# Reordering the opening of a filter-and-MLP kernel: filter spreads on VectorE, a fifth product on GpSimd, no filler matmuls, and M computed later

## The chip, the cores and the metric

The kernel runs on one core of one Trainium2 chip. The metric is the device time of an execution in microseconds (us). Lower is better. A profiled execution also gives a span, from its first instruction to its last, and times inside it are counted from the start of the span.

Engines are named as in the profile: PE is TensorE's matmul, PEld its weight load, DVE is VectorE, ACT is ScalarE, POOL is GpSimd, SP is SyncE.

## The reference

```python
# x (8, 3072, 256); filt_r, filt_i (1537, 256)
X = np.fft.rfft(x, axis=1)
Y = X * (filt_r + 1j * filt_i)[None]
y = np.fft.irfft(Y, n=3072, axis=1).reshape(24576, 256)
# w1, w2 (256, 1024); w_out (1024, 256)
g = np.maximum(y @ w1, y @ w2)
out = g @ w_out
```

Eight sequences are filtered along their length in the frequency domain, and every token of the result goes through a two-matrix maximum and an output matrix. All inputs and the output are float32.

## The kernel before

**The whole.** A transform of 3072 points is done as two short transforms by matrix products (128 points, called stage S1, then 24 points, S2), with a product by the filter between S2 and S3, and the way back as S3 and S4. The maximum is rewritten: `max(a, b) = relu(a - b) + b`, so the kernel needs `Wd = w1 - w2`, and `M = w2 @ w_out` for the part without the relu. The MLP takes tiles `tt` of 512 tokens, 6 for each of the 8 sequences. In the main loop (from line 719) each tile has eight steps; a step issues one hidden block (`moe_h`), one piece of the output of the tile before (`moe_o`), and what a table of steps (`plan`) puts there of the transforms of later sequences.

**The opening.** Before the main loop, lines 589 to 663 build the tables (sine tables `C1`, `G1`, `U`, `VP`, `VQ`; filter `F`; `Wd`, `M`) and transform sequence 0 without a trip through DRAM. The order there is written out by hand: a manual schedule keeps every engine's instructions in program order, and the engines wait for each other by semaphores. The change lies in this part alone. Its pieces:

- `load_f` brings the real (`ri` 0) and the imaginary (`ri` 1) half of the filter into `Fs`, by a DMA on POOL's queue. `expand_f(g, ri, E)`, a **spread**, copies group g of `Fs` by 8 to 12 matmuls into PSUM (`pf`), and engine E casts it into `F`. There are 8 groups with two halves each, 16 spreads.
- `first_s1(c, E)` is S1 for sixth c of the sequence: 8 matmuls into `pa`, evacuated by E into `At`. Before them come two **spins**, matmuls of zeros whose result nobody reads.
- `first_t1(g, V)` transposes part g of `At` into `pt`, and V (DVE) copies it to `bt`. It needs all six S1 tiles.
- `first_s2(g, pool)` makes two PSUM tiles `px` and multiplies both by `F` into `pq`, two products. DVE does both, or with `pool` set ACT copies the second tile to SBUF (`xs`) and POOL multiplies it.
- `first_s3(g, pq)` issues one spin and 32 small matmuls into `pz`, and ACT evacuates to `Zt`. With `split` ACT and DVE take half each.
- `tables_pe` (16 transposes of `U`, DVE copies to `VP`), `tables_q(h, S)` (`VQ` from `VP`), `table_g` (`G1` from `C1`), `fix_f` (POOL corrects group 0 of `F`).
- `prep_wd(k)` is POOL work: k 0 casts w2 to `w2b`, k 1 and 2 make the halves of `Wd`. `prep_w(k)` with k 0 and 1 transposes `w2b` into `w2T`; with k 2 and 3 it makes the halves of `M` in a PSUM tile `pm` by 8 matmuls each, and DVE evacuates `pm` after the second.
- `first_t2h(E, h)` transposes the first piece of `Zt` into `zr`; then `s4(0)`, line 661, needs `zr` and `G1`, and the main loop starts.

**PSUM.** In the opening two tags share it: `pa` with 2 slots of two banks, `px` with 4 slots of one bank. `bank2(...)` takes a `pa` slot. A spread for ACT takes one `pa` slot, a spread for DVE two `px` slots; `pt` of `first_t1`, `px` and the split `pz` take `px` slots. A matmul into a slot waits until its former tile has been read.

**The loop of the opening.** `order` is (1, 2, 3, 4, 5, 0, 6, 7). Pass n issues S2 of its group, the transposes of the group three passes on, a spread, and S3 of the group two passes back.

Of the kernel before, what the change touches and what calls it, by code (L numbers as in the profile page):

```python
# [8 lines left out]
FP32 = mybir.dt.float32  # L9
BF16 = mybir.dt.bfloat16  # L10
# [5 lines left out]
D = 256  # L16
# [13 lines left out]
def kernel(  # L30
# [26 lines left out]
    V, S, G, TE = nc.vector, nc.scalar, nc.gpsimd, nc.tensor  # L57
# [26 lines left out]
    p2 = setup.enter_context(tc.tile_pool(name="p2", bufs=2, space=bass.MemoryType.PSUM))  # L84
# [3 lines left out]
    def bank2(shape, dtype, name, tag=None):  # L88
        if tag is None:
            ring.append(ring.pop(0))  # L90
            tag = ring[-1]
        return p2.tile(shape, dtype, tag=tag, name=name)
# [20 lines left out]
    def expand_f(g, ri, E):  # L113
        if E is V:
            pf = [p2.tile([128, 2, D], FP32, tag="px", name="pf", bufs=4) for _ in range(2)]
        else:
            p_ = bank2([128, 2, 2, D], FP32, "pf")
            pf = [p_[:, b] for b in range(2)]
        fs = Fs[ri]
        for b in range(2):  # L120
            for c in range(2):
                m = 4 * b + c
                TE.matmul(pf[b][64 * c:64 * c + 32], Sel[:, m], fs[:, 2 * g:2 * g + 2], start=True, stop=True)
                p0 = 64 * c + 32
                if g:
                    TE.matmul(pf[b][p0:p0 + 32], Sel[:, 7 - m], fs[:, 16 - 2 * g:14 - 2 * g:-1], start=True, stop=True)  # L126
                else:
                    TE.matmul(pf[b][p0:p0 + 32, 0], Sel[:, 7 - m + c], fs[:, 0], start=True, stop=True)
                    TE.matmul(pf[b][p0:p0 + 32, 1], Sel[:, 7 - m], fs[:, 15], start=True, stop=True)
        f_ = F[:, ri, :, 2 * g:2 * g + 2].rearrange("p b u d -> p b (u d)")  # L130
        if E is V:
            for b in range(2):
                V.tensor_copy(f_[:, b], pf[b].rearrange("p u d -> p (u d)"))
        else:
            evac(E, f_, p_.rearrange("p b u d -> p b (u d)"))
# [145 lines left out]
    def sines_u(q):  # L281
        Uv = U.rearrange("p t (r x) -> p t r x", r=2)
        if q < 2:
            S.activation(Uv[:, :, :, 12 * q:12 * q + 12], uu[:, q], AF.Sin, bias=zero, scale=TWO_PI)
        else:
            for dr in range(2):
                S.activation(Uv[:, 0, dr, 0:24].rearrange("p (q j) -> p q j", q=2), uu[:, :, 0, dr], AF.Sin, bias=zero,
                             scale=mk[:, dr:dr + 1])
# [6 lines left out]
    def tables_pe():  # L295
        pv = bank2([128, 16, 2, 64], BF16, "pv")
        for u in range(16):
            TE.transpose(pv[:, u], U[:, 2 * u:2 * u + 2].rearrange("p c x -> p (c x)"), I128)
        V.tensor_copy(VP[:, :, :, 0:48], pv[:, :, :, 0:48])

    def table_g():
        pg = bank2([128, 128], BF16, "pg")
        TE.transpose(pg, C1, I128)
        S.activation(G1, pg, AF.Copy)

# [13 lines left out]
    def spin(pd, n):  # L319
        for _ in range(n):  # L320
            TE.matmul(pd, Sp, Sp.rearrange("p (o x) -> p o x", o=1).to_broadcast([128, 4, 128]), start=True, stop=True)

    def prep_wd(k, w1f, w2f):
        if k == 0:
            for dc in range(2):
                G.tensor_copy(w2b[:, dc], w2f[:, dc])
        else:
            G.tensor_tensor(Wd[:, k - 1], w1f[:, k - 1], w2f[:, k - 1], OP.subtract)
# [4 lines left out]
    pm_ = []  # L333

    def prep_w(k, E):
        if k < 2:
            pt = bank2([128, 4, D], BF16, "pt")
            for ji in range(4):
                for dc in range(2):
                    TE.transpose(pt[:, ji, 128 * dc:128 * dc + 128],  # L340
                                 w2b[:, dc, 128 * (4 * k + ji):128 * (4 * k + ji) + 128], I128)
            evac(E, w2T[:, 4 * k:4 * k + 4], pt)
            return
        if k == 2:
            pm_.append(bank2([128, 2, D], FP32, "pm"))
        for j in range(8):
            TE.matmul(pm_[0][:, k - 2], w2T[:, j, 128 * (k - 2):128 * (k - 2) + 128], Wo[:, j],
                      start=(j == 0), stop=(j == 7))
        if k == 3:
            evac(E, M, pm_[0])  # L350
# [88 lines left out]

    def first_s1(c, E):  # L440
        pa = bank2([128, 2, 2, 2, 4, T], FP32, "pa")
        spin(pa[:, 0].rearrange("p b a n t -> p (b a n t)"), 2)
        for dh in range(2):
            for n in range(4):
                TE.matmul(pa[:, dh, :, :, n], xb[0, c][:, n, 128 * dh:128 * dh + 128],
                          Ct.rearrange("p (b a t) -> p b a t", b=2, a=2), start=True, stop=True)
        evac(E, At[:, :, 0:48].rearrange("p h (a n) t -> p h a (n t)", a=2)[:, :, :, 128 * c:128 * c + 128],
             pa.rearrange("p h b a n t -> p (h b) a (n t)"))

    def first_t1(g, E):  # L450
        pt = p2.tile([128, 2, 2, D], BF16, tag="px", name="pt", bufs=4)
        t0 = 8 * (g // 2) + 2 * (g % 2)
        for c in range(2):
            for i in range(2):
                for dh in range(2):
                    TE.transpose(pt[:, c, i, 128 * dh:128 * dh + 128],
                                 At[:, 2 * dh:2 * dh + 2].rearrange("p b m t -> p t (b m)")[:, t0 + 4 * c + i], I128)
        o = bt[0][0:ROWS, 8 * (g // 2):8 * (g // 2) + 8].rearrange("p (c u) d -> p c u d", c=2)[:, :, 2 * (g % 2):2 * (g % 2) + 2]
        evac(E, o.rearrange("p c u d -> p c (u d)"), pt[0:ROWS].rearrange("p c u d -> p c (u d)"))

    def evac(E, out_, in_):
        if E is V:
            V.tensor_copy(out_, in_)
        else:
            S.activation(out_, in_, AF.Copy)  # L465

    def first_s2(g, pool):
        px = [p2.tile([128, 2, D], FP32, tag="px", name="px", bufs=4) for _ in range(2)]
        for i in range(2):
            for k, c in QUADS:  # L470
                t_ = 8 * (g // 2) + 4 * c + 2 * (g % 2) + i
                TE.matmul(px[k][64 * c:64 * c + 64, i], U[64 * k:64 * k + 48, 4 * g + 2 * i + c],
                          bt[0][64 * k:64 * k + 48, t_], start=True, stop=True)
        if pool:
            xs = apool.tile([128, 2, D], FP32, tag="at", name="xs")
            S.activation(xs[0:FROWS], px[1][0:FROWS], AF.Copy)
        pq = []
        for k in range(2):
            pq.append(pqpool.tile([128, 2, 2, D], BF16, tag="pq", name="pq"))
            E, src = (G, xs) if k and pool else (V, px[k])  # L480
            E.tensor_tensor(pq[k][0:FROWS],  # L481
                            src[0:FROWS].rearrange("p (o i) d -> p o i d", o=1).to_broadcast([FROWS, 2, 2, D]),
                            F[0:FROWS, :, k, 2 * g:2 * g + 2], OP.mult)
        return g, pq
# [115 lines left out]
    wf = load_w()  # L600
    load_wo()
    for c in range(6):
        load_x(1, c)
    spin(bank2([128, 2, 512], FP32, "pd")[:, 0], 24)
    order = (1, 2, 3, 4, 5, 0, 6, 7)
    expand_f(1, 0, S)
    expand_f(2, 0, S)
    first_s1(0, S)
    expand_f(3, 0, V)
    first_s1(1, S)  # L610
    sines_u(0)
    expand_f(4, 0, V)
# [4 lines left out]
    expand_f(0, 0, V)  # L617
    first_s1(4, V)
    first_s1(5, S)
    sines_u(2)  # L620
    first_t1(1, V)
    first_t1(2, V)
    expand_f(6, 0, S)
    table_g()
    tables_pe()
    expand_f(1, 1, S)
    first_t1(3, V)
    expand_f(2, 1, S)
    pend = []
    for n, g in enumerate(order):  # L630
        pend.append(first_s2(g, n in (0, 1, 3, 6)))
        if n < 5:
            first_t1(order[n + 3], V)
        if n < 6:
            expand_f((0, 3, 4, 5, 6, 7)[n], 1, S)
        if n in (1, 3):
            tables_q(n // 2, S)
        if n == 5:
            expand_f(7, 0, S)
        if n == 1:  # L640
            fix_f()
        if n in (3, 4, 6):
            prep_wd((3, 4, 6).index(n), *wf)
        if n > 5:
            prep_w(n - 6, V)
        if n > 1:
            first_s3(*pend.pop(0))
    prep_w(2, V)
    first_s3(*pend.pop(0))
    prep_w(3, V)  # L650
    first_s3(*pend.pop(0), split=True)
    zr[0] = zrpool.tile([128, N2, D], BF16, tag="zr", name="zr")
    first_t2h(V, 0)
    first_t2h(S, 1)
# [64 lines left out]
    for tt in range(6 * B + 1):  # L719
        b, i = divmod(tt, 6)  # L720
# [40 lines left out]
```

## Time and profile before

| | us |
|---|---|
| median of 6 runs | 539.84 |
| lowest, highest | 538.28, 543.79 |
| profiled execution, its own time | 538.28 |
| its span | 536.5 |
| opening, to the first matmul of `s4(0)` | 51.66 |
| main loop, from there to the end of the span | 484.84 |

The profiled execution is the fastest of the six, 1.56 us below the median, and 1.8 us of its own time lie outside the span. Busy shares of the whole span are PE 95%, ACT 63%, DVE 60% and POOL 14%. In the list of groups a row has the line, the engine, the operation, output and inputs with shapes, a count, busy time, mean ns of one, and the idle time ahead of them. In the timeline a row has a start, a duration, the engine, the line, and in brackets how long the engine had been idle and who released it.

### The profile page before, as it was taken

How to read it: one execution, taken by the hardware profiler on the slowest of the kernel's cores; microseconds unless marked ns; L12 is line 12 of the kernel's file. 1: busy time of each engine (PE TensorE's matmuls, PEld its weight loads, DVE VectorE, ACT ScalarE, POOL GpSimd, SP SyncE). 2: the span in 40 equal slices, each digit the busy share in tenths (PEclk: the TensorE clock that was granted, in tenths of full speed). 3: DMA queues.
4: the chain of work that ended last, by engine and by line, in shares of the span. 5: the costliest groups of instructions: out<-in, count | busy, mean ns of one | idle time of the engine just before them, and what ended most of it. 6: DMA issues, size and time to landing. Idle time of an engine off the chain costs nothing.

```text
span 536.5 us, 12166 instructions
## 1 busy us (share of the span) xinstructions
PE 510.8 (95%) x5135; PEld 347.1 (65%) x5213; DVE 323.5 (60%) x433; ACT 336.0 (63%) x594; POOL 74.7 (14%) x126
## 2 busy tenths in 40 slices
PE   8887999999999999999999899999999999999995
PEld 3545666666666666676667566676666666677774
DVE  8686679435863577438763677447863678443432
ACT  6685757865786578755775467755676556544540
POOL 7294011011101200021001200021000000000000
PEclk9999999999999999999999999999999999999998
DMA  8972496879678956699378966599367936421122
GB/s 156 285 131 42 142 174 147 200 237 196 138 233 215 202 155 176 172 223 210 99 228 199 199 148 163 159 222 220 115 188 205 159 106 160 118 89 77 42 80 79
DMA packets 67740, 87.06 MB, mean 162 GB/s; under 512 B 4002, under 2 KB 48292, under 8 KB 66596
## 3 DMA queue, kind: packets, MB, share of 16 engines
q1 hardware_dynamic: 52196, 44.84, 38.1%
q0 software_dynamic: 15488, 41.43, 29.3%
q8 instruction: 41, 0.67, 0.5%
q14 instruction: 15, 0.12, 0.1%
HBM read 53.74 MB, written 47.19 MB: 188 GB/s over the span
## 4 chain that ended last, share of the span: by engine, by line
PE 69%; DMA 5%; DVE 1%; issue 1%; ACT 0%; SPq 0%
PE po L572 27%; PE ph L547 23%; PE po L567 7%; PE pz L401 4%; DMA bt<-ad 3%; PE px L420 3%; PE py L531 3%; PE pa L366 3%; DMA ad<-at 2%; DVE pq L425 1%; ACT at L465 0%; DVE ot L574 0%; SPq L376 0%
## 5 line engine op out<-in xcount | busy, mean ns | idle before, releaser
L552 ACT ACTIVATE gt<-ph 128x512 bf16<-128x512 f32 x307 | 181.9, 599 | 110.4 <-PE ph L547 108.3
L572 PE MATMUL po<-Wo,gt 128*128 128x256 bf16 x1536 | 229.8, 273 | 3.2
L572 PEld LDWEIGHTS <-gt 128*128 128x128 bf16 x1536 | 150.2, 98 | 57.6
L425 DVE TENSOR_TENSOR pq<-px,F 120x1024 bf16<-120x1024 f32 x112 | 131.7, 1218 | 25.7 <-PE px L420 24.8
L574 DVE COPY ot<-po 128x512 f32<-128x512 f32 x96 | 66.2, 690 | 109.4 <-PE po L572 108.8
L405 ACT ACTIVATE zt<-pz 112x512 bf16<-112x512 f32 x112 | 60.7, 594 | 45.8 <-PE pz L401 40.7
L547 PEld LDWEIGHTS <-Wd 128*128 128x128 bf16 x768 | 69.9, 98 | 25.0 <-issue 10.7
L579 POOL DMA_DIRECT2D out_dram<-ot x47 | 25.2, 537 | 435.5 <-DVE ot L574 435.5
L550 DVE TENSOR_SCALAR gt<-ph 128x512 bf16<-128x512 f32 x77 | 52.9, 687 | 35.0 <-PE ph L547 27.4
L465 ACT ACTIVATE at<-pa 128x512 bf16<-128x512 f32 x78 | 46.8, 600 | 8.3 <-PE pa L366 6.4
L366 PE MATMUL pa<-xb,C 128*128 128x512 bf16 x83 | 31.1, 381 | 0.1
L531 PE MATMUL py<-G,zr 128*128 128x128 bf16 x384 | 29.7, 219 | 1.4 <-ACT zr L465 0.7
L401 PE MATMUL pz<-pq,VP 56*64 56x256 bf16 x448 | 28.8, 271 | 1.6 <-DVE pq L425 1.6
L531 PEld LDWEIGHTS <-zr 128*128 128x128 bf16 x384 | 24.9, 98 | 5.7 <-issue 2.9
L401 PE MATMUL pz<-pq,VQ 56*64 56x256 bf16 x448 | 28.1, 268 | 0.0
L101 POOL DMA_DIRECT2D xb<-in_x_dram x48 | 26.0, 552 | 8.6 <-PE pf L126 5.0
L420 PE MATMUL px<-bt,U 48*64 48x256 bf16 x448 | 23.8, 281 | 2.4 <-DMA bt<-ad 2.4
L420 PEld LDWEIGHTS <-U 48*64 48x64 bf16 x448 | 8.4, 104 | 14.6 <-issue 11.8
L465 ACT ACTIVATE F<-pf 128x1024 bf16<-128x1024 f32 x12 | 12.1, 1022 | 7.0 <-PE pf L126 6.8
L401 PEld LDWEIGHTS <-VP 56*64 56x64 bf16 x448 | 13.4, 106 | 3.7 <-DVE pq L425 2.2
L481 DVE TENSOR_TENSOR pq<-px,F 120x1024 bf16<-120x1024 f32 x12 | 14.3, 1219 | 2.0 <-ACT VQ L465 1.4
L401 PEld LDWEIGHTS <-VQ 56*64 56x64 bf16 x448 | 13.4, 107 | 0.0
(372 smaller groups left out, 576.1 us busy)
## 6 DMA issues: line engine op xcount, KB each, us to landing
out_dram<-ot POOLq DMA_DIRECT2D x47, 512.0 KB, 4.0
xb<-in_x_dram POOLq DMA_DIRECT2D x48, 256.0 KB, 7.8
ad<-at SPq DMA_DIRECT2D x42, 256.0 KB
bt<-ad SPq DMA_DIRECT2D x28, 384.0 KB
zd<-zt SPq DMA_DIRECT2D x56, 192.0 KB
zr<-zd SPq DMA_DIRECT2D x14, 768.0 KB
wf<-in_moe_w_dram POOLq DMA_DIRECT2D x2, 1024.0 KB, 14.9
Fs<-in_filt_r_dram POOLq DMA_DIRECT2D x1, 768.0 KB, 7.4
```

The lines of the kernel that those rows point to most:

```text
L366: TE.matmul(pa, C1, xb[b, c // 2][:, 2 * (c % 2):2 * (c % 2) + 2], start=True, stop=True)
L401: TE.matmul(pz[c][64 * k:64 * k + 64, i], W[64 * c:64 * c + 56, 2 * g + i, k], pq[k][64 * c:64 * c + 56, ri, i], start=(ri == 0), stop=(ri ...
L405: S.activation(zt[0:ROWS, c, o:o + 2], pz[c][0:ROWS], AF.Copy)
L420: TE.matmul(px[k][64 * c:64 * c + 64, i], U[64 * k:64 * k + 48, 4 * g + 2 * i + c], bt_[64 * k:64 * k + 48, t_], start=True, stop=True)
L425: V.tensor_tensor(pq[k][0:FROWS], px[k][0:FROWS].rearrange("p (o i) d -> p o i d", o=1).to_broadcast([FROWS, 2, 2, D]), F[0:FROWS, :, k, 2 ...
L465: S.activation(out_, in_, AF.Copy)
L531: TE.matmul(py[:, n], zr[b][:, 4 * i + n, 128 * dc:128 * dc + 128], G1, start=True, stop=True)
L547: TE.matmul(ph, Wd[:, dc, 128 * j:128 * j + 128], y_[:, dc].rearrange("p a b -> p (a b)"), start=(dc == 0), stop=(dc == 1))
L550: V.tensor_scalar(gt[tt][:, j], ph, 0.0, None, OP.max)
L552: S.activation(gt[tt][:, j], ph, AF.Relu)
L572: TE.matmul(p_, g_[:, jj, 128 * n:128 * n + 128], Wo[:, jj], start=False, stop=(jj == 7))
L574: V.tensor_copy(ot[tt][:, n - 1:n + 1], po[tt])
```

## The change

Eight edits, all in the opening:

1. The first spins, which run while the first filter half is loaded, are 20 instead of 24.
2. The two spins ahead of each of the six S1 tiles are gone.
3. The real spread of group 6 is issued right after S1, and DVE casts it instead of ACT. The real spread of group 7 moves from pass 5 to between the first transposes.
4. `tables_pe` and the imaginary spread of group 2 move from ahead of the first S2 to just behind it, in pass 0.
5. POOL does the second product of five passes (0, 1, 2, 4, 6) instead of four (0, 1, 3, 6).
6. `fix_f` moves from pass 1 to pass 2, and the three parts of `prep_wd` from passes 3, 4, 6 to 4, 6, 7.
7. The halves of `M` are issued one place later: the first between the last two S3 groups, the second behind the last one. `pm` takes a `px` slot instead of a `pa` slot.
8. `table_g` moves from ahead of `tables_pe` to the end, ahead of `first_t2h`, and takes a `px` slot.

```diff
     def table_g():
-        pg = bank2([128, 128], BF16, "pg")
+        pg = p2.tile([128, 128], BF16, tag="px", name="pg", bufs=4)
...
         if k == 2:
-            pm_.append(bank2([128, 2, D], FP32, "pm"))
+            pm_.append(p2.tile([128, 2, D], FP32, tag="px", name="pm", bufs=4))
...
     def first_s1(c, E):
         pa = bank2([128, 2, 2, 2, 4, T], FP32, "pa")
-        spin(pa[:, 0].rearrange("p b a n t -> p (b a n t)"), 2)
...
-    spin(bank2([128, 2, 512], FP32, "pd")[:, 0], 24)
+    spin(bank2([128, 2, 512], FP32, "pd")[:, 0], 20)
...
     first_s1(4, V)
     first_s1(5, S)
+    expand_f(6, 0, V)
     sines_u(2)
     first_t1(1, V)
     first_t1(2, V)
-    expand_f(6, 0, S)
-    table_g()
-    tables_pe()
+    expand_f(7, 0, S)
+    first_t1(3, V)
     expand_f(1, 1, S)
-    first_t1(3, V)
-    expand_f(2, 1, S)
     pend = []
     for n, g in enumerate(order):
-        pend.append(first_s2(g, n in (0, 1, 3, 6)))
+        pend.append(first_s2(g, n in (0, 1, 2, 4, 6)))
+        if n == 0:
+            tables_pe()
+            expand_f(2, 1, S)
         if n < 5:
             first_t1(order[n + 3], V)
         if n < 6:
             expand_f((0, 3, 4, 5, 6, 7)[n], 1, S)
         if n in (1, 3):
             tables_q(n // 2, S)
-        if n == 5:
-            expand_f(7, 0, S)
-        if n == 1:
+        if n == 2:
             fix_f()
-        if n in (3, 4, 6):
-            prep_wd((3, 4, 6).index(n), *wf)
+        if n in (4, 6, 7):
+            prep_wd((4, 6, 7).index(n), *wf)
         if n > 5:
             prep_w(n - 6, V)
         if n > 1:
             first_s3(*pend.pop(0))
+    first_s3(*pend.pop(0))
     prep_w(2, V)
-    first_s3(*pend.pop(0))
+    first_s3(*pend.pop(0), split=True)
     prep_w(3, V)
-    first_s3(*pend.pop(0), split=True)
+    table_g()
```

## The prediction

> **What bounds it now.** I read the page's busy shares first, then a table of stretches, then who waited for whom in the opening, then timelines of the single engines. The page says PE is busy 95% of the span. The stretches are cut at the first spread, the first transpose of `first_t1`, the first S2, the first half of `M`, and `s4(0)`; a row gives the length, then busy us (and instructions) of PE, PEld, DVE, ACT, POOL, then clock, DMA share and GB/s:
>
> ```profile
> PE 510.8 (95%) x5135; PEld 347.1 (65%) x5213; DVE 323.5 (60%) x433; ACT 336.0 (63%) x594; POOL 74.7 (14%) x126
> ```
>
> ```profile
> 0.00:9.37 9.37, 7.99 (x24) 2.97 (x25) 7.84 (x48) 5.92 (x12) 6.95 (x23) 1.00 0.69 131
> 9.37:20.27 10.90, 9.09 (x112) 5.00 (x112) 9.56 (x16) 8.64 (x10) 4.79 (x7) 1.00 1.09 224
> 20.27:25.90 5.63, 4.66 (x65) 3.03 (x66) 2.68 (x4) 2.75 (x5) 1.06 (x2) 1.00 1.08 365
> 25.90:45.74 19.84, 17.03 (x385) 10.01 (x383) 17.81 (x20) 16.51 (x20) 16.08 (x11) 1.00 0.56 99
> 45.74:51.66 5.92, 4.37 (x90) 3.16 (x90) 2.31 (x5) 1.90 (x3) 2.47 (x3) 1.00 0.56 88
> 51.66:536.50 484.84, 467.61 (x4464) 322.97 (x4539) 283.32 (x344) 300.22 (x545) 43.38 (x81) 1.00 0.67 163
> ```
>
> The reader sees that 484.84 us of the span are the main loop, which the change leaves alone; everything in it is placed by steps after `s4(0)`, so it moves with the opening's end. The opening from 9.37 to 51.66 has PE busiest, but DVE (9.56 of 10.90, then 17.81 of 19.84) and POOL (16.08) are close behind. The waits of PE there, in us, times and longest:
>
> ```profile
> PE pz L321 <- ACT F L465: 1.2, 2, 0.8
> PE pt L456 <- ACT At L465: 1.1, 1, 1.1
> PE pv L298 <- ACT F L465: 1.0, 1, 1.0
> PE pm L347 <- ACT Zt L507: 0.9, 1, 0.9
> PE pt L513 <- DVE Zt L463: 0.8, 1, 0.8
> PE pt L456 <- DVE pq L481: 0.3, 1, 0.3
> ```
>
> So PE's issue and short waits for evacuations share the path. The timelines give the pieces (start, duration):
>
> ```profile
> 12.92 2.47 DVE L133 CAST F<-pf 128x512 bf16<-128x512 f32 x4
> 18.35 1.22 DVE L463 CAST At<-pa 128x1024 bf16<-128x1024 f32 x1
> 36.36 2.36 DVE L481 TENSOR_TENSOR pq<-px,F 120x1024 bf16<-120x1024 f32 x2 [1.38 <-ACT VQ L465]
> ```
>
> ```profile
> 11.11 0.59 PE L321 MATMUL pa<-Sp 128*128 128x512 bf16 x2 [0.69 <-ACT F L465]
> 45.74 1.30 PE L347 MATMUL pm<-Wo,w2T 128*128 128x256 bf16 x8 [0.90 <-ACT Zt L507]
> 50.23 0.74 PE L513 MATMUL pt<-I,Zt 128*128 128x128 bf16 x8 [0.77 <-DVE Zt L463]
> ```
>
> ```profile
> 24.40 0.53 POOL L101 DMA_DIRECT2D xb<-in_x_dram x1 [1.80 <-PE pv L298]
> 27.62 4.26 POOL L481 TENSOR_TENSOR pq<-xs,F 120x1024 bf16<-120x1024 f32 x2 [2.69 <-ACT xs L476]
> 36.31 2.01 POOL L326 CAST w2b<-wf 128x1024 bf16<-128x1024 f32 x2
> ```
>
> DVE's first cast at 12.92 follows its table work without a gap; a cast takes 0.61, a POOL product 2.13. On PE I use start-to-start times: spread 0.55, S1 tile 0.54, pair of spins 0.44, transposes 0.65, S2 0.35, S3 with its spin 0.81, half of `M` 0.89, `tables_pe` 0.98.
>
> [...] 10 spins start before 5.0 us (0.43 each), later ones are 0.22 apart. The clock column reads 1.00 even then, so only matmul durations tell. [...] a DVE product beside a POOL product takes 1.22 as it does alone, so I charge nothing for sharing. [...]
>
> **The change, part by part.** I follow the lead, how much earlier PE reaches a point.
>
> *Start.* Four spins fewer: 0. The filter's DMA lands at 9.37 either way; PE waits 1.2 instead of 0.36 for it.
>
> *S1.* Twelve spins of 0.22 leave PE, 2.6 us. But DVE cannot start before 12.92: eight casts by 0.61 reach 17.8, the evacuation of tile 4 (1.22) 18.95. The transposes start at 19.1, not 20.27. ACT is done by 18.2 (two casts to 11.98, then five tiles by 0.92 and three sines, 2.3). Lead 1.2; the other 1.4 becomes PE waiting. Group 6's two casts (1.2) come next on DVE, delaying `bt` to 20.1; PE's spread of group 7 covers that.
>
> *To the first S2.* Two transposes, spread 7, a transpose (2.5) bring PE to 21.6. The imaginary filter half lands at 21.56 (issued 7.06, 14.5 us to landing), just in time. Spread, S2 at 22.2 instead of 25.90. Most of these 3.7 us only changes order: `tables_pe` and spread 2 now follow. The product waits for ACT's cast (23.2) and ends 24.4; behind it on DVE is the `VP` copy (0.96), until 25.3, and the next spread waits for that copy's slot. The second S2 comes at 26.0 instead of 27.44. Lead 1.45.
>
> *Passes 1 to 4.* Same work per pass. DVE loses 1.14 of product in pass 2, and PE's 0.3 wait for it goes; ACT gains one `xs` (0.52) in its slack. Lead 1.75.
>
> *Pass 5.* S2 of group 0 to S2 of group 6 took 2.92 (38.20 to 41.12). Without spread 7 and the waits around it (0.16 and 0.42): 0.35 + 0.55 + 0.81 + 0.15 = 1.85. Lead 2.8.
>
> *POOL.* Its queue opens after the last x load, 24.93. Products end at 27.1, 29.7 and 32.2 (the latter two wait for `xs` at 27.6 and 30.1), `fix_f` (2.44) at 34.7, the fourth product (its `xs` at 35.2) at 37.3, `w2b` (2.0) at 39.3. PE reaches the transposes of `w2b` at 41.47 − 2.8 = 38.7 and waits 0.7. Lead 2.1. Queued behind on PE are S3 of group 5 and S2 of group 7, and DVE's next products wait for that S2. `Wd` ends near 46.1, its first reader at 49: free. The loop's x loads behind it on POOL come about 1 us earlier.
>
> *`M`.* Before: wait 0.9, half of `M` 1.14, S3 0.81, half 0.89, S3 0.81. Now the first half follows S3 of group 6 without a wait, the second follows the last S3: 1.14 leaves the path, and 0.2 of wait for a `w2T` slot. Behind the last S3, 0.89 and `table_g` (0.08) stand where PE idled 0.77: 0.2 back. `M`'s evacuation (0.69) delays DVE's half of `zr`, but ACT's half (0.60) ends later anyway; `G1` (0.27) fits ACT's idle 1.03. Lead 2.1 + 1.14 + 0.2 − 0.2 = 3.2.
>
> No DMA moves on SP. Sum: `s4(0)` at 48.5, the profiled execution's own 538.28 becomes 535.1. It is the lowest of six, 1.56 under the median; the same step from the median gives 536.6.
>
> Unknown sizes: the S1 gain lies between 0 (a slot of `px` or the filter DMA holds PE) and 2.6 (PE alone); the POOL wait between 0 and 2 (one more product's delay, 2.1); `M` between 0.7 and 1.4. I take the middle values above. Lead 2.2 to 4.0 seems likely, 535.3 to 538.1 with half a us of scatter.
>
> **Rivals.** *POOL becomes the bound.* It works nearly without a pause from 24.9 to 46, and every product waits for ACT's `xs`. If each comes 0.5 later, `w2b` comes 2 us later, and `w2T`, both halves of `M` and S3 follow. Against it: today's products last 2.13 ± 0.01. Lead 1.2, time 538.6.
>
> *The clock falls.* Spins kept PE fed between S1 tiles. Without them PE waits 1.2 at 8.1 to 9.4, 0.7 at 10.4 and 1.6 ahead of the transposes. At half rate each us of PE work costs another. From 11.0 to 25.9 PE would hold 6.0 of S1 and spreads and 5.0 of the rest, 22 us for 14.9 of time: 7 late, against a lead of 3.2 about 3.8 slower, 543.6. It decides from some 10 us of half rate on (half of it lost, less 2 of PE's waits, eats 3.2). Against it: between 49.40 and 51.66 today PE is busy only 0.80 of 2.26, and the next 128x512 matmul still takes 0.38.
>
> *It doesn't do what it says.* The instruction order shows the five POOL products, so only a gain hidden again by the loop's DMA is left; its transfers are tied to steps, and I give that no chance of its own.
>
> **Numbers.** A measurement here tells about 0.5%, 2.7 us, from no change. Forecast 0.65 (0.57 beyond 2.7, 0.08 within), POOL 0.18 (0.03 beyond, 0.15 within), clock 0.17 (0.15 slower, 0.02 within): faster 0.60, same 0.25, slower 0.15. The time is 536.6. The low end, 534.9, is a lead of 4 with scatter; the high end, 540.4, takes in the POOL case and a short fall of the clock, and leaves out the long one.
>
> **What would show it.** `first_t1` near 19.1, second S2 near 26.0, a wait of PE for `w2b` near 38.7, the first half of `M` without its 0.9 wait, `s4(0)` near 48.5, and a main loop of 484.8. Spread matmuls above their 0.38 would show the clock. Wrong would be a lead that the loop gives back, or `w2b` past 41.

## The result, and the profile after

| | us |
|---|---|
| kernel before, median of 70 runs | 538.79 |
| changed kernel, median of 33 runs | 534.68 |
| ratio, 95% interval | 0.9921, 0.9908 to 0.9935 |
| forecast, range | 536.6, 534.9 to 540.4 |

The change is a gain of 4.1 us. The direction, faster by more than 0.5%, was forecast; the time lies 0.22 us below the range.

Two profiled executions of the changed kernel are shown. The first took 537.26 us, 2.6 above its kernel's median, and its TensorE clock fell for a while in the opening. The second (`e16_after_again3` below) took 533.69 us, and in it the clock held until the last few us of the program (mean 0.997), as in the profile of before (0.996). Busy shares of the first:

```profile
PE 508.7 (95%) x5119; PEld 346.0 (65%) x5197; DVE 323.6 (60%) x434; ACT 335.4 (63%) x594; POOL 77.2 (14%) x127
```

The shares say nothing: PE lost 16 instructions (12 spins and 4 first spins) out of 5135, and the percentages stand. The stretches, cut at the same events as before, do. First the execution with the fall:

```profile
9.09:20.04 10.95, 8.73 (x108) 4.46 (x108) 9.99 (x18) 8.61 (x10) 5.09 (x7) 0.84 1.09 216
20.04:22.93 2.89, 2.89 (x41) 1.91 (x42) 2.73 (x5) 1.49 (x3) 0.53 (x1) 1.00 1.01 390
22.93:44.50 21.57, 18.34 (x401) 10.72 (x399) 17.96 (x20) 16.94 (x21) 17.65 (x12) 1.00 0.68 140
44.50:49.10 4.60, 3.93 (x91) 3.26 (x91) 2.04 (x4) 2.17 (x4) 3.67 (x4) 1.00 0.19 14
49.10:535.50 486.40, 467.65 (x4464) 323.07 (x4539) 283.24 (x344) 300.23 (x545) 43.36 (x81) 1.00 0.67 163
```

And the execution without one, cut at 19.01 (`first_t1`) and 48.26 (`s4(0)`); its first row starts at 9.37 as before's does, 0.16 behind its own first spread:

```profile
9.37:19.01 9.64, 7.19 (x108) 3.86 (x101) 9.47 (x17) 8.66 (x10) 4.96 (x7) 1.00 1.12 219
...
48.26:531.90 483.64, 467.61 (x4464) 323.06 (x4539) 283.17 (x344) 300.36 (x545) 43.34 (x81) 1.00 0.67 164
```

The reader sees the clock of 0.84 in S1 of the first and 1.00 in the second; DVE busy for 9.47 of 9.64 us there; and a main loop whose busy time is the same to 0.1 us in all three profiles (467.6), while its length varies.

The waits of PE up to `s4(0)`, in the execution with the fall (engine, tile, line, what was waited for; total, times, longest):

```profile
PE pz L321 <- ACT Zt L506: 0.9, 1, 0.9
PE pa L444 <- DMA xb<-in_x_dram: 0.9, 1, 0.9
PE pt L340 <- POOL w2b L326: 0.8, 1, 0.8
PE pt L455 <- ACT At L464: 0.7, 1, 0.7
PE pf L123 <- ACT F L464: 0.5, 1, 0.5
```

The wait of `pm` for `Zt` (0.9) is gone. But a spin of S3 (`pz`) now waits 0.9 for the same evacuation, just before the first half of `M`. The wait for `w2b` is new and was forecast.

Timelines of the execution without a fall, PE, then POOL (start, duration, what, and in brackets the idle time before and its releaser):

```profile
19.01 1.24 PE L455 MATMUL pt<-I,At 128*128 128x128 bf16 x16 [0.69 <-ACT At L464]
22.08 0.41 PE L471 MATMUL px<-bt,U 48*64 48x256 bf16 x8
25.71 0.41 PE L471 MATMUL px<-bt,U 48*64 48x256 bf16 x8
39.43 0.56 PE L340 MATMUL pt<-I,w2b 128*128 128x128 bf16 x7 [0.76 <-POOL w2b L326]
44.22 1.05 PE L347 MATMUL pm<-Wo,w2T 128*128 128x256 bf16 x8
48.26 0.61 PE L530 MATMUL py<-G,zr 128*128 128x128 bf16 x8 [0.69 <-ACT zr L464]
```

```profile
29.89 2.15 POOL L480 TENSOR_TENSOR pq<-xs,F 120x1024 bf16<-120x1024 f32 x1 [0.31 <-ACT xs L475]
35.28 2.13 POOL L480 TENSOR_TENSOR pq<-xs,F 120x1024 bf16<-120x1024 f32 x1 [0.86 <-ACT xs L475]
37.36 2.02 POOL L326 CAST w2b<-wf 128x1024 bf16<-128x1024 f32 x2
```

`first_t1` starts at 19.01 (forecast 19.1), the first S2 at 22.08 (22.2), the second at 25.71 (26.0), the third product on POOL ends at 32.04 (32.2), the fourth near 37.4 (37.3), `w2b` at 39.38 (39.3), the wait for it is 0.76 (0.7), the first half of `M` has no wait of its own, and `s4(0)` starts at 48.26 (48.5). At 19.01 the bracket names ACT, whose last evacuation of S1 ends at 18.83; DVE's ends at 18.91. In e15 below ACT's ends at 18.67, DVE's at 18.91 again, and the transposes start at 19.01 again, so DVE now bounds S1. The step sum held at every mark. What it was subtracted from, and what happens in the other executions, is where the forecast failed.

### The profile page after: what moved, and what is told of

It is laid out like the page before. It is cut to its first block, busy times and chain, and to the rows that moved or that the text cites. A ratio compares the mean times of both kernels' runs of the same rounds, so it can differ in the third digit from the quotient of the medians.

```text
span 535.5 us, 12135 instructions
## 1 busy us (share of the span) xinstructions
PE 508.7 (95%) x5119; PEld 346.0 (65%) x5197; DVE 323.6 (60%) x434; ACT 335.4 (63%) x594; POOL 77.2 (14%) x127
## 3 DMA queue, kind: packets, MB, share of 16 engines
q1 hardware_dynamic: 52196, 44.84, 37.4%
## 4 chain that ended last, share of the span: by engine, by line
PE 70%; DMA 6%; DVE 1%; issue 1%; ACT 0%; SPq 0%
PE po L571 27%; PE ph L546 23%; PE po L566 7%; DMA bt<-ad 4%; PE pz L401 4%; PE px L420 3%; PE py L530 3%; PE pa L366 3%; DMA ad<-at 2%; DVE pq L425 1%; ACT at L464 0%; DVE ot L573 0%; SPq L376 0%
## 5 line engine op out<-in xcount | busy, mean ns | idle before, releaser
L464 ACT ACTIVATE F<-pf 128x1024 bf16<-128x1024 f32 x11 | 11.2, 1025 | 5.6 <-PE pf L126 4.8
```

## The experiments

**The lever that sorts the runs.** Each run comes with its mean granted clock. In the openings of the twenty profiles at hand (5 of the kernel before, 6 of the changed one, 9 of variants) half clock comes in stretches of 3.41 us or two of them in a row, called windows here. One window takes 0.5 × 3.41 / 535 = 0.0032 off the mean. The end of the span runs at half clock too, behind PE's last matmul: the last 4.5 us in the first profile of before, the last 3.4 in the first of after. The mean is 0.996 to 0.998 in the five profiles without a window in the opening, 0.993 to 0.995 in nine with one, 0.990 in three with two; e9 and e11, with one in the opening, have 0.991 and 0.992, and e1, with two, has 0.984. So I read 0.996 or more as no window, 0.993 to 0.995 as one, 0.990 to 0.992 as two, and less as more, which is an estimate from these profiles. Sorting the runs this way takes the clock out of a comparison. Medians in us, with counts in parentheses, over the runs of all the sets whose clocks are listed:

| kernel | no window | one | two | more |
|---|---|---|---|---|
| before | 537.65 (60) | 539.51 (49) | 540.95 (37) | 542.45 (16) |
| changed | 533.87 (21) | 535.43 (25) | 536.01 (12) | 539.99 (2) |
| changed, spins kept (e2) | 535.87 (9) | 536.59 (2) | 540.04 (1) | 540.85 (1) |
| changed, `M` as before (e9) | 535.21 (8) | 535.65 (5) | 538.77 (2) | |
| changed, POOL as before (e7) | 535.90 (1) | 535.38 (3) | 537.46 (1) | 537.50 (1) |
| changed, `w2b` earlier (e8) | 534.46 (11) | 534.80 (7) | 535.23 (2) | 537.44 (2) |
| changed, S1 fed again (e11) | 534.67 (7) | 536.19 (9) | 537.87 (4) | |
| before, spins gone (e3) | (0) | 537.50 (6) | 537.75 (5) | 539.74 (5) |
| before, `M` later (e4) | 536.68 (6) | 537.65 (5) | 539.38 (10) | 542.07 (1) |
| before, new order (e5) | 537.02 (5) | 538.31 (5) | 540.49 (3) | 542.49 (1) |
| before, new POOL work (e6) | 537.37 (7) | 539.59 (8) | 541.12 (6) | 547.00 (1) |

Changed against before: 3.8 us (95% interval 3.3 to 4.1) with no window, 4.1 (3.4 to 4.8) with one, 4.9 (4.3 to 5.8) with two. I worked out these intervals by redrawing the runs. Small counts are weak, and runs of different sets are pooled.

**The changed kernel again (e1).** No edit.

> The changed kernel once more, for a second profile and a paired time. The first profile showed half clock from 13.1 to 16.5 us and a main loop 1.6 us longer than before's. Theory 'steps' (the lead comes from the four parts of the change, 3.2 us in all, and the loop takes no part): without a fall of the clock first_t1 starts at 19.1 and s4(0) at 48.3 to 48.6, the loop lasts 484.8 to 486.4, time 0.994 of before. Rival 'loop' (the opening gives about 3, another us comes from the loop): loop below 484.5, time 0.992. Rival 'clock' (the fall belongs to the change and is there in most executions): half clock in this profile too, first_t1 at 20, s4(0) at 49.1.

Measured: 535.40 (22 runs) against 540.08 of the kernel before in the same set, ratio 0.9923 (0.9904 to 0.9942). The result repeats. Its profiled execution took 541.52 us. Two windows of half clock lie inside S1; its mean clock of 0.984 stands for 17.3 us at half clock in all, so that, with an end of 3.4 to 4.5, about two more fell in the main loop, by estimate. The time is 7.6 above the kernel's median without windows; 4.8 us of waits for the DMA of `bt` in the loop are part of that.

**Spins kept (e2).** The changed kernel with the spins of the kernel before.

```diff
+        spin(pa[:, 0].rearrange("p b a n t -> p (b a n t)"), 2)
...
-    spin(bank2([128, 2, 512], FP32, "pd")[:, 0], 20)
+    spin(bank2([128, 2, 512], FP32, "pd")[:, 0], 24)
```

> The changed kernel with the two spins ahead of each S1 tile and the 24 first spins put back. 'Steps': first_t1 back at 20.3, then 0.2 of it hidden later, s4(0) at 49.3 to 49.5, 0.9 us slower than the changed kernel, time 0.9955 of before. 'Clock': no half clock here, so as fast as the changed kernel or faster, and less scatter between runs.

Measured: 536.23 (13 runs), ratio 0.9947 (0.9921 to 0.9973). Undoing edits 1 and 2 costs 1.3 us in ratios against the same reference. In the band without a window it costs 2.0 (535.87 against 533.87; interval 1.2 to 2.8), where I had expected 0.9. In its profile S1 lost its clock for one window although the spins were there, so they are no guard.

**Spins gone alone (e3).** The kernel before with edits 1 and 2 only.

```diff
-        spin(pa[:, 0].rearrange("p b a n t -> p (b a n t)"), 2)
...
-    spin(bank2([128, 2, 512], FP32, "pd")[:, 0], 24)
+    spin(bank2([128, 2, 512], FP32, "pd")[:, 0], 20)
```

> The kernel before with only the spins changed (none ahead of S1 tiles, 20 at the start). 'Steps': first_t1 near 19.2, s4(0) at 50.6, 1.0 us faster than before, time 0.998. 'Clock': half clock for 3.4 us in the S1 stretch in the profile, first_t1 at 20 or later, no gain, 1.000.

Measured: 538.23 (16 runs), ratio 0.9972 (0.9952 to 0.9992). At an equal number of windows it gains 2.0 to 3.2, but not one of its 16 runs is free of windows (60 of 162 are before). Three stretches of its profile, PE busy first, then the clock as the last but two:

```profile
16.51:19.93 3.42, 1.91 (x28) 1.57 (x28) 2.41 (x5) 3.20 (x5) 1.06 (x2) 1.00 0.99 221
19.93:23.34 3.41, 2.44 (x30) 1.83 (x29) 1.28 (x2) 1.19 (x2) 0.53 (x1) 0.82 1.01 388
23.34:26.75 3.41, 3.41 (x40) 1.68 (x38) 1.65 (x2) 1.38 (x2) 0.53 (x1) 0.68 1.22 299
```

PE was busy 1.91 of 3.42 us around the end of S1, and the half clock comes after that, from about 22.1 (a clock of 0.82 is a third of the row at half), in `tables_pe` (1.84 us there, 1.05 at full clock), where PE is on the path. The order of the kernel before has no work for PE in that gap. The changed kernel puts two spreads there (groups 6 and 7), and 21 of its 60 runs are free of windows. A fall at this place, from 22.1 to 22.5, is in 3 of the 8 profiles with the old order (e3, e4, e20) and in none of the 12 with the new one. Two of the three, e4 and e20, have their spins, so taking the spins out is not needed for it. The gap as its cause, and with it that edits 2 and 3 belong together, is my estimate from these profiles, not shown.

**`M` later alone (e4).** The kernel before with edit 7.

```diff
-            pm_.append(bank2([128, 2, D], FP32, "pm"))
+            pm_.append(p2.tile([128, 2, D], FP32, tag="px", name="pm", bufs=4))
...
+    first_s3(*pend.pop(0))
     prep_w(2, V)
-    first_s3(*pend.pop(0))
+    first_s3(*pend.pop(0), split=True)
     prep_w(3, V)
-    first_s3(*pend.pop(0), split=True)
```

> The kernel before with only the halves of M one place later and pm in a px slot. 'Steps': PE's 0.9 wait ahead of the first half becomes a wait ahead of the S3 spin, the half itself leaves the path, s4(0) at 50.6, 1.0 us faster, time 0.998. Rival (DVE is late: M's evacuation ahead of DVE's half of zr delays s4): s4(0) at 51.3 or later, gain below 0.4, 0.9995.

Measured: 538.34 (22 runs), ratio 0.9973 (0.9954 to 0.9992); without a window 1.0 (0.4 to 1.7) faster than before.

**The new order alone (e5).** The kernel before with edits 3, 4 and 8: group 6 cast by DVE, group 7 early, `tables_pe` behind the first S2, `table_g` at the end.

```diff
+    expand_f(6, 0, V)
     sines_u(2)
...
-    expand_f(6, 0, S)
-    table_g()
-    tables_pe()
+    expand_f(7, 0, S)
...
+        if n == 0:
+            tables_pe()
+            expand_f(2, 1, S)
```

> The kernel before with only the reordering: group 6's real spread to DVE right behind S1, group 7's to ahead of the third transpose, tables_pe and spread 2 behind the first S2, table_g at the end. 'Steps': S2 of the second pass stays near 27 since DVE's VP copy and two casts now hold it, spread 7 leaves pass 5, s4(0) 0.6 earlier, time 0.9988. Rival (the order is worth what the first S2 shows, 3 us): time 0.995.

Measured: 538.14 (14 runs), ratio 0.9988 (0.9959 to 1.0017): not told from no change. Without a window it is 0.6 (0.4 to 1.7) faster.

**New POOL work alone (e6).** The kernel before with edits 5 and 6.

```diff
-        pend.append(first_s2(g, n in (0, 1, 3, 6)))
+        pend.append(first_s2(g, n in (0, 1, 2, 4, 6)))
...
-        if n == 1:
+        if n == 2:
             fix_f()
-        if n in (3, 4, 6):
-            prep_wd((3, 4, 6).index(n), *wf)
+        if n in (4, 6, 7):
+            prep_wd((4, 6, 7).index(n), *wf)
```

> The kernel before with only POOL's part: five products, fix_f one pass later, w2b, Wd one later. 'Steps': PE no longer waits 0.3 for DVE in pass 2, w2b lands near 40.5 just as PE asks for it, s4(0) 0.5 earlier, time 0.999. Rival (POOL is the bound): PE waits for w2b, no gain or a loss, 1.000 to 1.002.

Measured: 539.59 (22 runs), ratio 1.0004 (0.9983 to 1.0025). Nothing beyond 0.3 in any band with more than one run.

**POOL as before in the changed kernel (e7).** The e6 diff taken back.

> The changed kernel with POOL's work as in the kernel before: products of passes 0, 1, 3 and 6 only, the correction of F in pass 1, the parts of Wd in passes 3, 4 and 6. Undoes edits 5 and 6. Theory 'POOL's edits bring nothing' (alone they gave a ratio of 1.0004): no wait of PE for w2b, DVE one product more (1.2 us) in pass 2, s4(0) within 0.5 of the changed kernel's for the same clock, median 534.3 to 535.3. Rival 'they bring half a us or more once the rest is in' (my sum had 0.5): 535.5 to 536.5.

Measured: 536.04 (6 runs), ratio 0.9947 (0.9926 to 0.9967), an interval that overlaps the changed kernel's. Its profile has one window in S1, as two of the changed kernel's do whose `s4(0)` is at 48.12 and 48.29; here it is at 48.55. The wait for `w2b` is gone, and this stands in its place:

```profile
PE pt L340 <- DVE w2T L462: 1.1, 1, 1.1
```

The product that POOL no longer takes delays DVE, and DVE's evacuation of `w2T` is late instead. POOL's edits exchange 1.1 of one wait for 0.8 of another. They are worth some 0.3 in that comparison of profiles, and are not resolved in times.

**`w2b` earlier (e8).** The changed kernel with the cast of w2 one pass earlier, to take away the wait for it.

```diff
-        if n in (4, 6, 7):
-            prep_wd((4, 6, 7).index(n), *wf)
+        if n in (3, 6, 7):
+            prep_wd((3, 6, 7).index(n), *wf)
```

> The changed kernel with w2b cast one pass earlier (pass 3 instead of 4, ahead of POOL's fourth product). 'Steps': PE's 0.75 wait for w2b goes, the S3 that follows then waits for POOL's product or for ACT instead; 0.3 us faster than the changed kernel, 0.9917 of before. Rival (POOL's wait was the whole hold): 0.7 us faster, 0.991. If the fourth product comes late instead, the same as the changed kernel, 0.9923.

Measured: 534.73 (22 runs), ratio 0.9927 (0.9907 to 0.9948), the changed kernel's time. `s4(0)` stood at 48.10 with a full clock in the opening, 0.16 earlier than in the changed kernel, for this reason:

```profile
PE pt L340 <- DVE w2T L462: 0.6, 1, 0.6
```

The POOL wait of 0.8 turned into a DVE wait of 0.6. No variant of the study beats the changed kernel.

**S1 fed again (e11).** The changed kernel with one spin ahead of the S1 tiles 1 to 5 and five ahead of group 6's spread, ten in the place of twelve, set where PE waits.

```diff
+        if c:
+            spin(pa[:, 0].rearrange("p b a n t -> p (b a n t)"), 1)
...
+        if (g, ri) == (6, 0):
+            spin(pf[0].rearrange("p u d -> p (u d)"), 5)
```

> The changed kernel with ten spins put back where PE waits anyway: one ahead of each of S1 tiles 1 to 5 and five ahead of group 6's spread. By the steps these cost nothing, first_t1 stays at 19.1 when the clock is full. Theory 'clock' (falls of the clock to half for whole windows of 3.4 us, [...] cost time in most executions of both kernels): no fall between 13 and 20 us in the profile, median 0.5 to 1 us below the changed kernel's, 0.990 to 0.9915 of before. Rival (the falls lie in PE's slack and cost nothing, or the spins do not prevent them): 0.9923 as the changed kernel.

Measured: 535.54 (20 runs), ratio 0.9945 (0.9921 to 0.9970); 0.8 slower than the changed kernel without a window, and 7 of 20 runs without one, as in the changed kernel (21 of 60). Feeding PE between the tiles does not keep the clock and costs time.

**`M` as before in the changed kernel (e9).** The e4 diff taken back.

> The changed kernel with both halves of M back in their old places, in a pa slot: undoes edit 7 alone. My sum gave M 1.14: the median would then be 535.6 to 536.0, and 535.0 where no stretch of half clock fell (the changed kernel: 533.9). Theory 'M is worth more than its matmuls (alone it gave 1.5 in medians)': 536.2 to 536.6. Rival 'beside the other edits M is worth less, since S3 then waits for the evacuation of Zt instead': 534.9 to 535.4. In the profile the first half of M waits 0.5 to 0.9 again for an evacuation by ACT, and s4(0) is 1.0 to 1.3 later than the changed kernel's.

Measured: 535.36 (15 runs), ratio 0.9929 (0.9907 to 0.9950). Without a window 1.3 slower than the changed kernel (0.7 to 1.7), with one 0.2. In its profile `s4(0)` is at 49.42. That profile has a half-clock window in S1 (from 11.1 to 14.5), so it is set beside e15 and e17 below, which have one too: 1.30 and 1.13 later (1.16 against the full clock of e16). The first half of `M` waits 0.9 again:

```profile
PE pm L347 <- ACT Zt L506: 0.9, 1, 0.9
```

The 1.14 of my sum for `M` stands in the profile; the overall median alone, and the band with one window, would have said less.

**More profiles of both kernels.** No edits; e14 had the numbers of e13, e17 and e18 those of e16, e20 those of e19.

> The kernel before, unchanged, for a second profile. Theory 'clock windows come to both kernels': a stretch of half clock of 3.4 or 6.8 us shows somewhere in its first 50 us, s4(0) then at 52 to 53 where the first profile (none in its opening) had 51.66, and the profiled execution takes 539 to 541. Rival 'the spins between S1 tiles keep the clock up': full clock through the opening again, s4(0) at 51.5 to 51.9.

> The changed kernel, unchanged, for a third profile. Theory: the lead stands without regard to the clock's fall: s4(0) at 48.1 to 48.6 if the clock holds in the opening, 49.0 to 49.8 with a stretch of half clock. Rival 'the fall costs this kernel less than the kernel before, so that the lead grows in executions with a fall': s4(0) at most 49.0 with a fall, where the kernel before with a fall is 52.5 or more.

> The changed kernel once more, for a profile. Theory 'the step sum was right to the opening's end and the rest is in the loop': without a stretch of half clock s4(0) is at 48.0 to 48.6, and the loop takes 484.0 to 485.0. Rival 'the opening gains more than the sum': s4(0) at 47.0 to 47.7 with a full clock. With a stretch of half clock inside S1: s4(0) at 48.1 to 49.2.

> The kernel before once more, for a profile with a stretch of half clock in its opening (six in ten of its runs have a mean clock that says so; its three profiles have none). Theory 'a stretch inside S1 costs the kernel before 0.9 or more, since PE bounds S1 there': first_t1 at 21.0 to 21.6 and s4(0) at 52.3 to 53.0, where the changed kernel with one such stretch stood at 48.1 to 49.1. Rival 'it is hidden here too': s4(0) at 51.4 to 51.9 with a stretch of half clock. With a full clock: 51.4 to 51.7, and the question stays open.

| profile | its time | half clock in the opening | `first_t1` | `s4(0)` | loop | loop waits of PE for `bt` |
|---|---|---|---|---|---|---|
| before, first | 538.28 | none | 20.27 | 51.66 | 484.84 | 2.4 |
| e13, before | 537.35 | none | 20.15 | 51.53 | 484.06 | 1.9 |
| e14, before | 537.73 | none | 20.09 | 51.47 | 484.37 | 2.3 |
| e19, before | 539.49 | 3.41, in S1 | 21.64 | 53.03 | 484.70 | 1.9 |
| e20, before | 539.82 | 6.83, behind S1 | 20.09 | 53.92 | 484.13 | 2.1 |
| after, first | 537.26 | 3.41, in S1 | 20.04 | 49.11 | 486.35 | 4.1 |
| e15, after | 535.07 | 3.41, in S1 | 19.01 | 48.12 | 485.19 | 3.2 |
| e16, after | 533.69 | none | 19.01 | 48.26 | 483.67 | 1.6 |
| e17, after | 534.93 | 3.41, in S1 | 19.18 | 48.29 | 484.87 | 2.8 |
| e18, after | 535.80 | 6.83, in S1 | 21.12 | 50.20 | 483.81 | 1.8 |

Without a window the opening is 3.2 to 3.4 us shorter. The rival of e13 is out only with e19: the spins between S1 tiles did not keep the clock there. How one window in S1 can cost 1.5 at `s4(0)` in one kernel and nothing in the other is read from DVE's timelines. Kernel before, e19, half clock from 11.2 to 14.6 by the clock column of stretches of 1 us:

```profile
13.11 1.29 DVE L133 CAST F<-pf 128x512 bf16<-128x512 f32 x2
15.43 1.29 DVE L133 CAST F<-pf 128x512 bf16<-128x512 f32 x2 [1.02 <-PE pf L126]
16.96 1.29 DVE L133 CAST F<-pf 128x512 bf16<-128x512 f32 x2 [0.24 <-PE pf L126]
18.50 1.29 DVE L133 CAST F<-pf 128x512 bf16<-128x512 f32 x2 [0.26 <-PE pf L129]
19.71 1.22 DVE L463 CAST At<-pa 128x1024 bf16<-128x1024 f32 x1
```

Changed kernel, e15, half clock from 11.0 to 14.4:

```profile
12.91 4.87 DVE L133 CAST F<-pf 128x512 bf16<-128x512 f32 x8
17.69 1.22 DVE L462 CAST At<-pa 128x1024 bf16<-128x1024 f32 x1
```

Before, PE at half clock issues spins, tiles and spreads too slowly, and DVE waits 1.5 us in three places (0.5 in two places in the first profile of before, with a full clock). After, with 12 spins fewer, PE has that time to spare: eight casts run without a gap, and the transposes start at 19.01 as with a full clock. Before, a pair of spins inside the window took 0.83, start to start, instead of 0.45, ahead of a tile that was late already. In the first profile of after the window lay later (13.2 to 16.6, the last tiles of S1), and `s4(0)` was 0.9 later; but PE had waited 0.86 for the DMA of `xb` ahead of that window and was 0.7 behind e16 already, so the 0.9 isn't the window's alone. Two windows (e18) cost 1.9.

A window that costs nothing at `s4(0)` is not one that costs no time: e15 and e17 took 1.2 to 1.4 longer than e16, because their loops waited 1.2 to 1.6 longer for `bt`. Whether the window brings that wait isn't shown; e8, without a window, waited 3.9. The table leaves out e1, whose loop took 490.00, by the estimate above with two windows in it.

## Why the forecast was right in direction and outside its range

Step by step, with the profiles without a window (e16 for after, e13 and e14 beside the first of before):

- *Start, 0.* In time it was 0: the filter's landing sets the first spread. But PE now waits longer for it, 0.95 to 2.0 in the changed kernel's profiles against 0 to 1.15 before. Over all twenty profiles a half-clock window in S1 came in none of the 6 with a wait up to 0.9, and in 11 of the 14 with more. This is no proof that the four spins taken away bring windows into S1: three of the 11 (e2, e6, e19) have the 24 first spins. The wait also goes with the time at which the spacing of the first spins falls from 0.43 to 0.22, and that differs between executions: the same 24 spins took 7.99 in the first profile of before and 7.00 in e19, and PE then waited 0.36 and 1.15. I didn't try 24 first spins alone. My reading of the first spins was short as well: in the first profile of before 13 start at half clock, up to 6.12, not 10, and the spacing of 0.22 begins at 6.48.
- *S1, lead 1.2.* Right: 19.01 against 20.09 to 20.27. DVE bounds it, as worked out, though ACT was done at 18.83 in e16, not by 18.2. The spins' worth in times, 2.0 in e2, have an interval (1.2 to 2.8) that just takes in the 1.2.
- *To the second S2, 1.45; passes 1 to 5, 2.8.* The second S2 was at 25.71 (26.0), and PE reached the transposes of `w2b` at 38.45 (38.7). The order alone gave 0.6 in runs without a window (e5; interval 0.4 to 1.7, 5 runs), which tells no more than that these terms are of the right size.
- *POOL, a wait of 0.7.* Right: 0.76. The rival "POOL becomes the bound" is out: the products kept their 2.13 to 2.16, and `w2b` ended at 39.38. But e7 and e8 show that behind this wait stands one of DVE's, so that neither the edit nor its mending moves the end by more than some 0.3.
- *`M`, 1.14 and two times 0.2.* Right in sum: 1.1 to 1.3 in e9's profile. In detail the 0.9 wait moved to the spin of S3 ahead, where I had written that the first half follows S3 without a wait.
- *Loop unchanged, 484.8.* Right on average: 484.8 over the five changed profiles of the table, 484.4 over the five of before. Single executions differ by up to 2.7 us, and it is PE's wait for `bt`'s DMA that differs: length less that wait is 482.0 to 482.8 in all ten. On average the wait is 2.7 after and 2.1 before, so that a small part of the lead may go back in the loop; five profiles of each are too few to tell.

```profile
PE px L420 <- DMA bt<-ad: 4.1, 2, 2.4
```

```profile
PE px L420 <- DMA bt<-ad: 1.6, 2, 0.9
```

These are the loops of the first profile after and of e16.

So the lead of 3.2 is what a full clock gives up to `s4(0)`: 51.47 to 51.66 less 48.26 is 3.2 to 3.4. The step that failed is **"the same step from the median gives 536.6"**. It failed in two ways.

First, the base. The median of six, 539.84, was 1.05 above the one of 70 runs, 538.79. This term alone makes up more than half of the 1.9 us by which 536.6 missed 534.68. Many runs don't settle a base either: in e1's set the median of 60 runs of the same kernel was 540.08, with 18 of them free of windows, and in e5's set the median of 65 was 538.80, with 30 free. The profiled execution's own time gave 535.1, and by its clock it was no lucky exception, as I took it, but one of the nearly four runs in ten (60 of 162) without a window.

Second, the size: 4.1 between medians for 3.2. I carried a lead read from an execution with a full clock over to a median of executions of which more than six in ten have half-clock windows. By the medians of the table, most of the excess is there without a window: 3.8 (3.3 to 4.1), against 3.2 to 3.4 between the openings. That difference is inside the interval and stays open. Windows add to it: the first costs 1.9 before and 1.6 after, the second 1.4 and 0.6. An estimate from the profiles: weighted by the shares of runs with no, one and more windows (0.37, 0.30, 0.33 before; 0.35, 0.42, 0.23 after), `s4(0)` is at 52.8 before and 48.8 after, a lead of 4.0. It takes every window to lie in the opening, where most of those in the profiles were, leaves the loop out, and rests on few profiles. So the base is shown; that windows make the rest of the miss is argued.

The rival "the clock falls" named a fall that does come, and had its sign wrong. It took PE's path as the bound in S1, so that each us at half clock costs another, and took the fall as something that the change brings. The fall is there in both kernels, 3.4 or 6.8 us long in their openings, short of the 10 from which it was to decide, and the edit that was to bring it, taking spins out, gave PE slack that can absorb one window (e15). That a lack of PE work brings the fall was my assumption. Two stretches of the first profile after:

```profile
9.69:13.10 3.41, 1.85 (x32) 0.91 (x22) 3.27 (x7) 2.85 (x3) 1.69 (x3) 1.00 1.12 203
13.10:16.51 3.41, 3.41 (x32) 1.34 (x30) 2.75 (x5) 2.78 (x3) 1.98 (x3) 0.51 1.18 221
```

PE was busy 1.85 of 3.41 us, and the next stretch ran at half clock. The edges of these stretches lie within 0.1 us of the fall itself. In e8 the same stretch holds 1.89 us of PE's work, and no fall followed:

```profile
9.69:13.10 3.41, 1.89 (x30) 1.10 (x27) 3.27 (x7) 2.65 (x3) 1.12 (x3) 1.00 1.11 198
13.10:16.51 3.41, 3.27 (x53) 1.94 (x52) 3.41 (x6) 3.31 (x4) 1.66 (x3) 1.00 1.17 219
```

What brings a window or spares one isn't shown.

## What to carry to other kernels

Before a lead read from one profile is subtracted from a median, look at the mean clock of every run and count the half-clock windows in the profile and in the runs: executions with one window took 1.9 us longer before and 1.6 after, by the medians, and a window can fall on work that the change has moved off the path. Little PE work in a stretch does not tell whether half clock follows: it did after 1.85 of 3.41 us in the first profile of after, and did not after 1.89 in e8. Filler matmuls that stood in front of bounding work took nearly twice as long in a half-clock window of e19 (0.83 for a pair instead of 0.45); without them one window in S1 left `s4(0)` where it was in two profiles of three. A wait that is taken away is worth only what stands behind it: three edits here exchanged one wait of 0.6 to 1.1 us for another.

## What the runs showed that I had not expected

- TensorE ran at half its clock for windows of 3.41 us, or two of them, in more than six in ten executions of both kernels by their mean clocks (102 of 162 before, 39 of 60 after), and in the openings of 15 of the twenty profiles; in e1, by estimate, in the main loop too. Much of the spread of a kernel's times goes with this: medians of before go from 537.65 without a window to 542.45 with three or more.
- Two executions of the same program can differ by 2.5 us in one DMA wait alone (1.6 and 4.1 for `bt`).
